# Three block loads on one ring, and TensorE's padding moved from ahead of its dummy transposes into the MLP steps

## The chip, the cores and the metric

The kernel runs on one core of a Trainium2 chip. The metric is the device time of one execution in microseconds; several executions are timed and their median is compared. The engines are named as in the profile: PE is TensorE's matmul, PEld its weight load, DVE is VectorE, ACT is ScalarE, POOL is GpSimd, and SP is SyncE, which here only issues DMAs.

## The reference

A layer normalisation feeds two branches. The first is attention with 32 heads over the last 512 rows of a key and value cache, the second a two-layer MLP with a squared ReLU, whose output goes through a SiLU and gates the first.

```
xn = layernorm(x)                                  # x: 2048 x 640
s  = softmax(q(xn) @ k.T / sqrt(128)) @ v @ wo      # 32 heads, 512 cached rows
h  = relu(xn @ w1 + b1) ** 2                        # 640 -> 1728
g  = silu(h @ w2 + b2)                              # 1728 -> 640
return x + s * g
```

## The kernel before, in words

Every product of float32 values is made of three matmuls: each operand is split into a rounded high part and the rest, and high by high, high by low and low by high are added up in PSUM. The 2048 rows are cut into four tiles of 512, and a tile into four blocks of 128 rows.

**The first tile** (`ln_first`, L226 to L334) loads its four blocks `xb` straight from `x` and normalises them before anything else can run. Block 0 is cut in two halves, one issued by SP and one by ACT. Blocks 1 to 3 go to SP, ACT and SP in turn (L242). The DMAs that an engine issues follow one another on that engine's ring. DVE takes the blocks' statistics in order (`bn`, `aggr`); the reciprocal root of blocks 0 and 1 is found together on ACT, DVE and POOL, then that of blocks 2 and 3. PE turns the blocks, 20 transposes `px` in all, so that ACT and DVE can split them into `xT`, the MLP's moving operand. Until the first of these PE has nothing to do, and runs `WARM` dummy transposes `pw` of an identity matrix.

**The MLP** runs over `steps`, one for each tile (of the first three) and each of 14 chunks of the 1728 hidden columns. `mlp_step(n)` (L471) emits first the up product of step n (`up`, or `up_half` for the one chunk of 64 columns), then the down product of step n - 1 (`down`). A full up product has 15 matmuls and so has a full down product, so that the order on PE is up 0, up 1, down 0, up 2, down 1, and so on. Within the first up product stands one more transpose, `pb`, of the biases.

**Attention** follows from about 290 us on, in 128 units of half a fetch block each, written out by a plan of due times. Its matmuls are not touched by the change.

**Slots.** PE's instructions stand in its stream in numbered slots, one each. A matmul takes two, for its weight load and for itself; a wait on a semaphore that stands on its own takes one. `pe.addr_align(BLOCK, s)` puts NOPs into the stream when the program is loaded, as many as are needed until the next instruction's slot number is s modulo `BLOCK`, 256. That is from 0 to 255 of them. There are five such places in each attention unit (`align`, L1021), and one at the very front: L249 brings the first dummy transpose to slot 88. What stands ahead of the kernel's first instruction counts too, and is not in the kernel's own text. `Ordered` (L69) keeps what is issued through `pe`, `dve`, `act`, `pool` and `sp` in program order.

Of the kernel before, what the change touches and what calls it, by code (L numbers as in the profile page):

```python
# [14 lines left out]
P = 128  # L15
NT = 512
EPS = 1e-5
WARM = 40
BLOCK = 256
FIRST_SLOT = 188  # L20
SLOTS = (0, 11, 22, 33, 42)
LEAD_SLOT = 88


@with_exitstack
def kernel(
# [20 lines left out]
    DC = D // P  # L47
# [3 lines left out]
    LN_AT = {t: (3, 7) if t == LATE else (5, 9) for t in range(1, NTILE)}  # L51
# [12 lines left out]
    chunks = [(f0, min(P, F - f0)) for f0 in range(0, F, P)]  # L64
# [4 lines left out]
    class Ordered:  # L69
# [13 lines left out]
    pe, dve, act, pool, sp = (  # L83
        Ordered(e) for e in (nc.tensor, nc.vector, nc.scalar, nc.gpsimd, nc.sync)
    )
# [8 lines left out]
    def raw(ap):  # L94
        return ap.bitcast(F32)
# [39 lines left out]
    def ln_tile(t, b):  # L135
        tag = "stage" if b < 2 else "mr"
        return xp.tile([P, D], F32, tag=tag, name=f"xb{t}_{b}")
# [3 lines left out]
    def ln_load(t):  # L141
        mv = xp.tile([P, 4, NB], F32, tag="mv", name=f"mv{t}")[:, :2, :]
        sc = xp.tile([P, 3, NB], F32, tag="sc", name=f"sc{t}")
        xn = []
        for b in range(NB):
            xb = ln_tile(t, b)
            r0 = t * NT + b * P
            nc.sync.dma_start(xb, x[r0 : r0 + P, :])
            xn.append(xb)
        LS[t] = mv, sc, xn  # L150

    def ln_block(t, b):
        mv, sc, xn = LS[t]
        st = xp.tile([P, 2, 6], F32, tag="st", name=f"st{t}_{b}", bufs=4)
        hd = D // 2
        for i in range(2):
            dve.bn_stats(st[:, i, :], xn[b][:, i * hd : (i + 1) * hd])
        dve.bn_aggr(mv[:, :, b], st)

    def ln_var(t):  # L160
        mv, sc, xn = LS[t]
        dve.tensor_scalar(sc[:, 0, :], mv[:, 1, :], EPS, None, op0=ALU.add)
        nc.scalar.activation(sc[:, 1, :], sc[:, 0, :], AF.Sqrt)

    def ln_root(t):
        mv, sc, xn = LS.pop(t)
        var, sd, y = (sc[:, i, :] for i in range(3))
        r = mv[:, 1, :]
        dve.reciprocal(y, sd)
        dve.tensor_tensor(r, y, y, op=ALU.mult)  # L170
        dve.tensor_tensor(r, r, var, op=ALU.mult)
        dve.tensor_scalar(r, r, -0.5, 1.5, op0=ALU.mult, op1=ALU.add)
        dve.tensor_tensor(r, r, y, op=ALU.mult)
        return mv
# [21 lines left out]
    def ln_chunk(t, bc, xs, c):  # L196
        xc = xp.tile([P, D], F32, tag="stage", name=f"xc{t}_{c}")[:, :NT]
        nc.sync.dma_start(xc, xT[c * P : (c + 1) * P, t * NT : (t + 1) * NT])
        dve.tensor_tensor(xc, xc, bc[0], op=ALU.subtract)
        nc.vector.tensor_tensor(xc, xc, bc[1], op=ALU.mult)  # L200
        nc.scalar.activation(xs[0][:, c, :], xc, AF.Copy)
        nc.vector.tensor_tensor(xs[1][:, c, :], xc, raw(xs[0][:, c, :]), op=ALU.subtract)
# [23 lines left out]
    def ln_first():  # L226
# [3 lines left out]
        n = NB // 2  # L230
# [7 lines left out]
        xn = [ln_tile(0, b) for b in range(NB)]  # L238
# [1 line left out]
            js = slice(i * hd, (i + 1) * hd)  # L240
            q.dma_start(xn[0][:, js], x[:P, js])
        for b in range(1, NB):  # L242
            (sp if b % 2 else act).dma_start(xn[b], x[b * P : (b + 1) * P, :])
        act.activation(warm, warm, AF.Sqrt)
        br = xp.tile([P, P], F32, tag="br", name="br", bufs=1)
        dve.memset(br, 0.0)
        BR.append(br)
        pw = psx.tile([P, NT], F32, tag="x", name="pw")
        pe.addr_align(BLOCK, LEAD_SLOT)  # L249
        for _ in range(WARM):  # L250
            pe.transpose(pw[:, :P], ident, ident)
        pts = [ps_y.tile([P, NT], F32, tag="py", name=f"px0_{c}") for c in range(DC)]
# [83 lines left out]
    def spill(t, xs, cs=slice(0, DC)):  # L336
        for i in range(2):
            pool.dma_start(xT_d[t][i][:, cs, :], raw(xs[i])[:, cs, :])

    def load_part(f, k, held=False):  # L340
        f0, n = chunks[f]
        if f % 3 and f < 9:
            if k == 0:
                BOTH[f] = keep.tile([P, 2, D], F32, tag="acc", name=f"wr{f}", bufs=2)
            w = BOTH[f][:, k, :]
        else:
            w = xp.tile([P, D], F32, tag="stw", name=f"w{k + 1}r{f}", bufs=2)
            if held:
                dve.memset(w[:, :1], 0.0)
        if k == 0:  # L350
            w = w.rearrange("p (c n) -> p c n", n=P)[:, :, :n]
            sp.dma_start(w, w1[:, f0 : f0 + n].rearrange("(c p) f -> p c f", p=P))
        else:
            for i in range(0, P, n):
                sp.dma_start(w[i : i + n, :], w2[f0 : f0 + n, :])
        PRE[f, k] = w
# [14 lines left out]
    def split_w(f, k):  # L371
        if f < FC:
            split_hi(f, PRE[f, k], k)
            split_lo(f, PRE[f, k], k, dve)
            if 9 <= f < FC - 1:
                load_part(f + 1, k)
# [37 lines left out]
    def up(t, f, xs):  # L414
        if chunks[f][1] < P:
            return up_half(t, f, xs)
        ph = ps_h.tile([P, NT], F32, tag="ph", name=f"ph{t}_{f}")
        if t == 0 and f < 2:
            order = [(c, i, j) for c in range(3) for i, j in ((0, 0), (0, 1))]
            order += [(0, 1, 0), (1, 1, 0), (3, 0, 0), (3, 0, 1), (2, 1, 0), (3, 1, 0)]  # L420
            order += [(4, 0, 0), (4, 1, 0), (4, 0, 1)]
        else:
            order = [(c, i, j) for c in range(DC) for i, j in ((0, 0), (0, 1), (1, 0))]
        for k, (c, i, j) in enumerate(order):
            nc.tensor.matmul(  # L425
                ph,
                w1s[f][i][:, c, :],
                xs[j][:, c, :],
                start=k == 0,
                stop=k == len(order) - 1,  # L430
            )
            if t == f == 0 and k == 9:
                biases()
        r = hp.tile([P, NT], F32, tag="r", name=f"r{t}_{f}")
        if t == 0 and f == rp + 1:
            split_w(f + 1, 0)
        engines(t)[1].activation(r, ph, AF.Relu, bias=b1_sb[:, f : f + 1])
        hs = [hp.tile([P, NT], F32R, tag=f"h{i}", name=f"h{t}_{f}_{i}") for i in range(2)]
        square_split(t, f, r, hs[0], hs[1])
        return hs  # L440

    def down(t, f, hs, py):
        n = chunks[f][1]
        for d in range(DC):
# [4 lines left out]
            else:  # L449
# [5 lines left out]
                )  # L455

    xs_next = ln_first()
    steps = [(t, f) for t in range(LATE) for f in range(FC)]
    XS, HS, PY, LN = {0: xs_next}, {}, {}, {}

    def gate(t, tiles):
        for d in range(DC):
# [5 lines left out]
            )  # L468
            nc.gpsimd.dma_start(g_d[t][:, d, :], sg)

    def mlp_step(n):  # L471
        if n < len(steps):
            t, f = steps[n]
            ln_stats_at, ln_chunk_at = LN_AT[t + 1]
            if t == 0 and f == 1:
                ln_load(1)
            if t == 0 and f == 6:
                LN[1] = ln_root(1)
            if t and f == ln_stats_at - 1:
                ln_load(t + 1)  # L480
            if t and f == ln_stats_at:
                for b in range(NB):
                    ln_block(t + 1, b)
                ln_var(t + 1)
                LN[t + 1] = ln_root(t + 1)
            c = f - ln_chunk_at
            if 0 <= c < DC:
                ln_chunk(t + 1, *LN[t + 1], c)
                XS[t + 1] = LN[t + 1][1]
            if t + 1 == LATE and 0 < c <= DC:  # L490
                spill(t + 1, XS[t + 1], slice(c - 1, c))
            if t == 0 and f > 0:
                split_w(f, 1)
                if f < 8:
                    for k in range(2):
                        load_part(f + 2, k)
            HS[n] = up(t, f, XS[t])
            if t == 0 and 2 <= f < 2 + NB:
                ln_block(1, f - 2)
                if f == NB + 1:  # L500
                    ln_var(1)
            if f == ln_stats_at + 2:
                LN[t + 1] = ln_rows(t + 1, LN[t + 1])
            if t > 0 and f == 1:
                spill(t - 1, XS[t - 1])
            if t == LATE - 1 and f == 3:
                spill(t, XS[t])
        if n > 0:
            t, f = steps[n - 1]
            if f == 0:  # L510
                PY[t] = [
                    ps_y.tile([P, NT], F32, tag="py", name=f"py{t}_{d}") for d in range(DC)
                ]
            down(t, f, HS.pop(n - 1), PY[t])
            if f == FC - 1 and t < LATE - 1:
                gate(
                    t,
                    lambda d: xp.tile(
                        [P, D], F32, tag=("stage", "mr")[d % 2], name=f"sg{t}_{d}"
                    )[:, :NT],  # L520
                )
# [417 lines left out]
    for n in range(steps_n):  # L939
# [24 lines left out]
    q_hi(0)  # L964
    q_lo(0)
    mlp_step(steps_n)
    gate(
        LATE - 1,
# [133 lines left out]
    for item in order:  # L1102
        kind, n = item[0], int(item[1:] or 0)
# [125 lines left out]
```

## Time and profile before

| what | value |
|---|---|
| median of 3 runs | 1960.47 us (1960.15 to 1961.4) |
| the profiled execution | 1961.36 us, of which the span from the first to the last instruction is 1959.6 us |
| PE busy | 1951.1 us, 100% of the span |
| granted TensorE clock, mean | 1.000 |
| PE's weight loads, matmuls | 8616, 8616 |
| fetches of instructions (queue q8) | 77, 1.26 MB |

The page gives, for every engine, busy time and share; the span cut in 40 slices; the chain of work that ended last; and the costliest groups. The timeline lists instructions in order of time: start, duration, engine, line, operation, and in brackets how long the engine had been idle and what ended that. Instructions of a sequencer (NOPs and waits on semaphores) show up under their source line, with the engine's name and a q: PEldq is what PE's sequencer did by itself. The view of a window gives an engine's busy time and the granted clock in it.

### The profile page before, as it was taken

The numbers are of one execution on the slowest core, as the hardware profiler recorded it, in microseconds if no ns is written. First come the engines' busy times: TensorE is split into PE (matmuls) and PEld (weight loads), VectorE is DVE, ScalarE is ACT, GpSimd is POOL, SyncE is SP. The second block draws the span as 40 slices with busy tenths as digits, with TensorE's granted clock in tenths as the row PEclk, the third lists the DMA queues.
The fourth block names the chain that finished last, engine by engine and source line by source line (L and its number), as shares of the span: only waits on it lengthen the run. The fifth ranks groups of instructions, "written<-read, shape, count | busy, mean of one in ns | idle before, by whom it ended". The sixth has DMA issues, their size and how long they took to land.

```text
span 1959.6 us, 28181 instructions
## 1 busy us (share of the span) xinstructions
PE 1951.1 (100%) x8616; PEld 1611.8 (82%) x8616; DVE 1534.8 (78%) x2638; ACT 1187.1 (61%) x2039; POOL 1375.7 (70%) x757
## 2 busy tenths in 40 slices
PE   9999999999999999999999999999999999999998
PEld 7888888888888888888888888888888888888887
DVE  5633337788888888888888878888888888888865
ACT  4432336766666666666666676666666666666643
POOL 2121226888888888888887888888888888888841
PEclk9999999999999999999999999999999999999999
DMA  5330454333333232223335433443333333333353
GB/s 182 94 119 28 183 198 128 98 93 92 92 92 92 92 92 93 92 92 93 92 92 174 145 119 108 114 114 114 113 114 114 114 114 114 98 92 92 85 189 118
DMA packets 127892, 219.13 MB, mean 112 GB/s; under 512 B 23452, under 2 KB 38086, under 8 KB 126470
## 3 DMA queue, kind: packets, MB, share of 16 engines
q1 hardware_dynamic: 124598, 202.43, 34.1%
q0 software_dynamic: 2864, 14.42, 1.8%
q8 instruction: 77, 1.26, 0.2%
q14 instruction: 65, 0.53, 0.1%
q10 hardware_dynamic: 288, 0.49, 0.1%
HBM read 193.41 MB, written 23.87 MB: 111 GB/s over the span
## 4 chain that ended last, share of the span: by engine, by line
PE 98%; DMA 1%; DVE 1%; POOL 0%; ACT 0%; issue 0%; SPq 0%; POOLq 0%; ACTq 0%
PE r L77 22%; PE pq L77 22%; PE o L77 18%; PE s L77 18%; PE ph L425 7%; PE ly L77 2%; PE py L101 2%; PE py L100 2%; PE py L102 2%; PE lu L77 2%; PE eu L77 0%; PE ph L396 0%; POOL pt L77 0%; DMA xb<-in_x_dram 0%; PE py L448 0%; PE py L447 0%
## 5 line engine op out<-in xcount | busy, mean ns | idle before, releaser
L77 POOL TENSOR_TENSOR pt<-e,pt 128x1024 fp32r<-128x1024 f32 x256 | 615.5, 2404 | 115.2 <-ACT pt L77 69.1
L77 PE MATMUL r<-ot,wo 128*128 128x512 f32 x1920 | 496.6, 389 | 0.0
L77 PE MATMUL pq<-ax,wq 128*128 128x512 f32 x1920 | 456.1, 389 | 0.0
L77 PEld LDWEIGHTS pq<-ax,wq 128*128 128x128 f32 x1920 | 360.3, 188 | 75.3 <-DVE q L77 0.4
L77 PEld LDWEIGHTS r<-ot,wo 128*128 128x128 f32 x1920 | 360.4, 188 | 74.9
L77 PE MATMUL o<-pt,wv 128*128 128x512 f32 x1536 | 369.7, 389 | 0.1
L77 PE MATMUL s<-q,wk 128*128 128x512 f32 x1536 | 369.1, 389 | 0.1
L77 DVE TRANSPOSE_TENSOR_REDUCE rdm<-s 128x16 f32<-128x512 f32 x512 | 346.5, 711 | 6.2 <-PE s L77 6.0
L77 ACT ACTIVATE e<-e 128x1024 f32<-128x1024 f32 x256 | 269.8, 1054 | 125.5 <-DVE e L77 82.0
L77 PEld LDWEIGHTS o<-pt,wv 128*128 128x128 f32 x1536 | 288.1, 188 | 60.9 <-POOL pt L77 1.2
L77 PEld LDWEIGHTS s<-q,wk 128*128 128x128 f32 x1536 | 288.1, 188 | 60.5 <-DVE e L77 0.7
L77 DVE TENSOR_TENSOR e<-s,bm 128x512 f32<-128x512 f32 x512 | 312.2, 664 | 7.6 <-DMA bm<-m_d 7.1
L77 POOL TENSOR_TENSOR su<-e,e 128x1024 f32<-128x1024 f32 x128 | 309.1, 2415 | 0.0
L77 ACT ACTIVATE pt<-e 128x1024 fp32r<-128x1024 f32 x256 | 272.0, 1063 | 6.9
L77 DVE TENSOR_TENSOR acc<-r,acc 128x512 f32<-128x512 f32 x300 | 203.4, 678 | 12.9 <-PE r L77 12.6
L77 ACT ACTIVATE rdm<-rdm 32x64 f32<-32x64 f32 x384 | 97.8, 255 | 181.5 <-DVE rdm L77 178.4
L77 DVE TRANSPOSE_TENSOR_REDUCE rds<-su 128x32 f32<-128x1024 f32 x128 | 158.3, 1237 | 0.3 <-POOL su L77 0.3
L77 DVE TENSOR_TENSOR ot<-o,ot 128x512 fp32r<-128x512 f32 x128 | 88.5, 691 | 86.1 <-ACT ot L77 86.1
L77 ACT ACTIVATE q<-pq 128x512 fp32r<-128x512 f32 x128 | 76.7, 600 | 111.5 <-PE pq L77 111.4
L425 PE MATMUL ph<-xT,w1s 128*128 128x512 f32 x585 | 139.5, 390 | 0.0
L425 PEld LDWEIGHTS ph<-xT,w1s 128*128 128x128 f32 x585 | 109.5, 188 | 23.5 <-DVE xT L77 0.9
L77 ACT ACTIVATE rds<-rds 32x32 f32<-32x32 f32 x384 | 89.7, 234 | 63.0 <-DVE rds L77 59.7
(137 smaller groups left out, 1940.9 us busy)
## 6 DMA issues: line engine op xcount, KB each, us to landing
bm<-m_d SPq DMA_DIRECT2D x128, 256.0 KB, 3.2
bs<-s_d SPq DMA_DIRECT2D x128, 256.0 KB, 4.0
qr<-in_wq_dram SPq DMA_DIRECT2D x64, 320.0 KB, 4.5
or<-in_wo_dram SPq DMA_DIRECT2D x64, 320.0 KB, 4.7
kr<-in_kT_dram SPq DMA_DIRECT2D x64, 256.0 KB, 4.3
vr<-in_v_dram SPq DMA_DIRECT2D x64, 256.0 KB, 4.4
xT_d<-xT POOLq DMA_DIRECT2D x6, 1280.0 KB, 8.0
ax<-xT_d SPq DMA_DIRECT2D x4, 1280.0 KB, 10.6
```

The costliest lines, as they stand in the source:

```text
L77: ins = method(*args, **kwargs)
L100: nc.tensor.matmul(ps, ah, bh, start=first and i == 0, stop=False)
L101: nc.tensor.matmul(ps, ah, bl, start=False, stop=False)
L102: nc.tensor.matmul(ps, al, bh, start=False, stop=last and i == n - 1)
L425: nc.tensor.matmul(ph, w1s[f][i][:, c, :], xs[j][:, c, :], start=k == 0, stop=k == len(order) - 1,)
```

## The change

Blocks 2 and 3 are now issued by SP right behind block 1, so that ACT issues only its half of block 0. The alignment ahead of the dummy transposes is gone, and `WARM` is 38 in place of 40. In steps 1 to 23 of the MLP there is a new alignment behind the step's up product and ahead of the down product. The slot that it asks for is a start, `LEAD_SLOTS`, plus two slots for each matmul that `up` and `down` and the row transposes have emitted by then, plus `LEAD_PADS` for each step.

```
-WARM = 40
+WARM = 38
-LEAD_SLOT = 88
+LEAD_SLOTS, LEAD_PADS = 171, 2
...
         for b in range(1, NB):
-            (sp if b % 2 else act).dma_start(xn[b], x[b * P : (b + 1) * P, :])
+            sp.dma_start(xn[b], x[b * P : (b + 1) * P, :])
...
-        pe.addr_align(BLOCK, LEAD_SLOT)
         for _ in range(WARM):
             pe.transpose(pw[:, :P], ident, ident)
...
+    LEAD_N = 23
+
+    def lead_slot(n):
+        ups = sum(2 * (2 if chunks[steps[k][1]][1] < P else 3) * DC for k in range(n + 1))
+        downs = sum(2 * (2 if chunks[steps[k][1]][1] < P else 3) * DC for k in range(n - 1))
+        turns = 2 * sum(1 for k in range(n + 1) if steps[k][1] == LN_AT[steps[k][0] + 1][0] + 2)
+        return (LEAD_SLOTS + ups + downs + turns + LEAD_PADS * n) % BLOCK
...
             if t > 0 and f == 1:
                 spill(t - 1, XS[t - 1])
+            if 0 < n <= LEAD_N:
+                pe.addr_align(BLOCK, lead_slot(n))
             if t == LATE - 1 and f == 3:
                 spill(t, XS[t])
```

## The prediction

> **What bounds the kernel now.** I read the page first: busy times and the chain that ended last.
>
> ```profile
> span 1959.6 us, 28181 instructions
> ...
> PE 1951.1 (100%) x8616; PEld 1611.8 (82%) x8616; DVE 1534.8 (78%) x2638; ACT 1187.1 (61%) x2039; POOL 1375.7 (70%) x757
> ...
> PE 98%; DMA 1%; DVE 1%; POOL 0%; ACT 0%; issue 0%; SPq 0%; POOLq 0%; ACTq 0%
> ```
>
> PE is the bound, almost without a gap. Whatever keeps PE waiting is added to the time as it is, and little is to be gained. The waits of PE's weight loads from 20 us to the end say how little:
>
> ```profile
> PEld o L77 <- POOL pt L77: 1.2, 3, 0.5
> PEld s L77 <- DVE e L77: 0.7, 2, 0.6
> PEld py L101 <- DVE h L77: 0.5, 1, 0.5
> PEld pq L77 <- DVE q L77: 0.4, 1, 0.4
> ```
>
> That is 2.8 us in seven waits (us in total, times, longest). The rest of what PE loses lies before its first real work, in the first 20 us. The timeline there:
>
> ```profile
> 2.55 6.51 PE L77 MATMUL pw<-ident 128*128 128x128 f32 x40 [2.55 <-issue]
> 3.54 0.89 DVE L77 BATCH_NORM_STATS2 st<-xb 128x6 f32<-128x320 f32 x2 [2.50 <-DMA xb<-in_x_dram]
> ...
> 4.62 0.06 DVE L77 MEMSET w1r<- 128x1 f32 x1
> ...
> 5.56 0.89 DVE L77 BATCH_NORM_STATS2 st<-xb 128x6 f32<-128x320 f32 x2 [0.88 <-DMA xb<-in_x_dram]
> ...
> 8.51 0.83 ACT L77 ACTIVATE xb<-xb,mv 128x640 f32<-128x640 f32 x1 [0.76 <-POOL mv L77]
> ...
> 9.39 0.53 PEld L77 LDWEIGHTS px<-ident,xb 128*128 128x128 f32 x5 [0.56 <-ACT xb L77]
> ```
>
> DVE has block 0's statistics done at 4.68, waits 0.88 us for block 1 to land, and the chain from there (statistics, root, scale) frees PE's first transposes at 9.39. The 40 dummies end at 9.06, 0.33 us ahead of that.
>
> **The loads.** What the DMAs moved in the first 14 us, in 40 slices of 0.35 us:
>
> ```profile
> GB/s 0 0 0 0 0 124 234 304 410 377 307 388 410 410 410 293 129 110 227 344 364 399 355 135 89 219 168 209 401 399 354 322 337 389 432 395 432 351 359 402
> ```
>
> The sixth to the sixteenth slice move 1283 KB (their sum, 3667 GB/s, by 0.35 us), so all four blocks of 328 KB land close together at about 5.6 us. In one ring's order block 1 is complete when 656 KB have moved. The slices reach 614 KB at 3.85 us and 750 KB at 4.2, so it lands at about 4.0 to 4.3, before DVE asks for it at 4.68. The 0.88 us go. Block 0 no longer shares with block 2 and may come up to 0.4 us sooner too. Against it: one ring might move less than two, and then nothing is gained. Bounds 0 to 1.3 us, taken 0.9, since from slice 20 on SP alone moves as much. Blocks 2 and 3 cannot come later than 5.8 us, where the four are complete, and DVE takes block 2 at 5.9 in the new order. ACT's issue of block 2 (0.4 us) goes and SP's of block 3 comes as late again; SP's next one, the first weights, waits for DVE's memset at 4.62 anyway, so nothing waits for either.
>
> **The padding in front.** What PE's sequencer did by itself, from its rows under line 77 up to 20.5 us, and then over the whole span:
>
> ```profile
> L77 PEldq NOP  x23: 13/13/13, 0.8 to 2.5; - x23
> L77 PEldq EVENT_SEMAPHORE  x5: 51/51/51, 7.0 to 14.8; - x5
> ```
> ```profile
> L77 PEldq NOP  x2528: 13/13/13, 0.8 to 1855.1; - x195
> ```
>
> 23 NOPs stand ahead of the dummies, from 0.8 to 2.5 us (the load behind them starts at 2.52): 0.074 us each. Without them the dummies start when POOL has made the identity, at about 1.35, and 38 of them end near 7.6 to 8.0. That is before the transposes, now due at 8.5, so the front padding costs nothing before, and its removal and two dummies fewer bring nothing.
>
> **Where the new alignments fall.** This decides. The 23 NOPs brought the stream to slot 88, so the kernel's first free slot was 88 - 23 = 65. Nothing in the change alters what stands ahead of it. Now count the slots to the first new alignment, step 1's, between the second up product and the first down product: 65, then 76 for 38 dummies, 40 for 20 transposes, 30 for the first up product, 2 for `pb`, 30 for the second, and 5 for the semaphore waits in the row above: 248. The slot asked for is 171 + 30 + 30 (`ups` for steps 0 and 1) + 0 + 0 + 2 = 233. The stream is 15 slots beyond it, and the next slot 233 is 241 NOPs away. Counted on in the same way, the other 22 alignments need one or two each, 41 together, and attention starts at the same slot as before, one block of 256 later.
>
> The 41 cost 41 x 0.074 = 3.0 us of PE's sequencer and I cost them at nothing: the other 2505 NOPs of the row above lie among the matmuls of attention, where all of PE's waits are the 2.3 us above. What covers them is the sequencer's lead, which these rows show at the place of the first alignment:
>
> ```profile
> L100 PEld LDWEIGHTS py<-h,w2s x5: 187/188/188, 19.8 to 22.9; 128*128 128x128 f32 x5
> L100 PEldq EVENT_SEMAPHORE  x1: 51/51/51, 16.4 to 16.4; - x1
> ```
> ```profile
> L425 PEld LDWEIGHTS ph<-xT,w1s x20: 187/188/192, 15.3 to 19.6; 128*128 128x128 f32 x20
> ```
> ```profile
> 23.77 3.56 PE L425 MATMUL ph<-xT,w1s 128*128 128x512 f32 x15
> ```
>
> The semaphore wait in front of the first down load was passed at 16.4 us, the load itself ran at 19.8. A matmul takes (3.56 - 0.39) / 14 = 0.226 us, so the sequencer was 15 matmuls, 3.4 us, ahead. If that cover were gone everywhere the 41 would cost their 3.0 us.
>
> 241 NOPs are 241 x 0.074 = 17.8 us, five times the lead. Bounds for one NOP, from the row's rounding, 0.070 and 0.078, hence 16.9 to 18.8.
>
> **The sum.** The sequencer comes to the padding at 16.4 - 0.9 = 15.5 us, leaves it at 33.3, and the first down load runs at 33.4 in place of 19.8: +13.6. PE has run dry at 18.9, and stands for 14.5 us. Behind it all of PE's work, and so everything else, is later by the same amount. DVE, ACT and POOL go on meanwhile, so the wait for `h` is over:
>
> ```profile
> 20.00 0.39 PE L100 MATMUL py<-h,w2s 128*128 128x512 f32 x1
> ...
> 20.44 0.50 PE L101 MATMUL py<-h,w2s 128*128 128x512 f32 x1
> ...
> 20.77 0.40 PE L102 MATMUL py<-h,w2s 128*128 128x512 f32 x1
> ```
>
> These three started 0.77 us apart where 0.45 would do: -0.3. Last, the clock. Rows of the dummies before and after 6.4 us, PE's last matmuls, and the end of the span:
>
> ```profile
> L77 PE MATMUL pw<-ident 128*128 128x128 f32 x18 | 4.1, 422 | 2.5 <-issue 2.5
> ```
> ```profile
> L77 PE MATMUL pw<-ident 128*128 128x128 f32 x22 | 2.6, 277 | 0.0
> ```
> ```profile
> 1947.76 6.74 PE L77 MATMUL ly<-lh,l2w 128*128 128x512 f32 x29
> ```
> ```profile
> 1956.00:1959.60 3.60, 0.00 (x0) 0.00 (x0) 0.68 (x2) 0.00 (x0) 0.00 (x0) 0.92 0.21 73
> ```
>
> The first 18 dummies follow each other at (4.1 - 0.42) / 17 = 0.216 us, the other 22 at (2.6 - 0.28) / 21 = 0.110: for about 4.0 us from its first matmul PE ran at half speed. The last matmul ends at 1954.5, and in the last 3.6 us the granted clock averages 0.92: at half speed for 0.6 us, so it fell some 4.5 us after the last work. An idle time of 14.5 us is thus long enough for it to fall, and 4.0 us at half speed cost about 4.0 x 0.49 = 1.9 us. Bounds: 0, and 3.3 for a cold time as long as all 40 dummies' 6.5.
>
> [...]
>
> 13.6 - 0.3 + 1.9 = +15.2 us. Against the profiled execution, 1961.36 (1.76 us of it outside the span), that is 1976.6; it stood 0.9 above the median of 1960.47, against which I forecast 1975.7.
>
> **The rivals.**
> The padding is short (the other side). It turns on 15 slots: had the stream at step 1 reached slot 233 or less, the alignment would take 0 to 2 NOPs or so, as the other 22 do, and what is left is the gain of 0.9: 1959.6, no change that can be told. For it: what stands ahead of the kernel was counted in a profiled execution, and the timed ones may have 15 fewer; the pads of the other steps are all small, as if the start of 171 had been taken for such a stream. Against it: nothing in the trace shows a first slot other than 65.
> The padding is passed faster than the front's NOPs were. Between the waits at 14.8 and 16.4 the sequencer passed 43 slots in 1.65 us, 0.038 each. At that pace 241 take 9.2 us, the first down load runs at 24.8, +5.0 - 0.3, and with the clock 1967.1; jumped over at once they would leave 1959.6. Against it: the front's row, three times as slow or more, for the same instruction.
> [...]
> The clock stays up: 1973.8. One ring brings nothing: 1976.6. Both lie within the likeliest case's range.
>
> **How the numbers follow.** The long padding at the front's pace has 0.83. The short padding has 0.12; padding passed faster 0.04, half of it slower and half unchanged; 0.01 is left for a gain elsewhere. 0.2% is 3.9 us, about what a measurement of this kernel can tell from no change, and a gain of 0.9 is far below that, so faster 0.01, same 0.14, slower 0.85. The low end takes 0.9 less for the NOPs, 0.4 more for the loads and no clock loss, 1972.5; the high end 1.0 more for the NOPs, 0.9 for no gain from the loads, 1.4 for the clock and a run like the slowest shown (0.9), 1979.9. The short padding is left outside, as the 2 in 10 allow.
>
> **What would show it.** Under line 77 no NOPs before the dummies, which start near 1.35 us; DVE's idle before block 1's statistics gone; transposes from about 8.5. In the MLP 282 NOPs (under line 77, the helper's), 241 of them in one run from about 15.5 to 33.3 us; PE idle from about 19 to 33.4, the granted clock at half behind that for some 4 us, and from there the same spacing as before. 2505 or 2506 NOPs in attention, 78 fetches on q8. It would be wrong if the kernel's first slot is 50 or lower, which shows as a first alignment of no more than two NOPs.

## The result and the profile after

The changed kernel takes 1976.16 us in the median of five runs (1975.17 to 1977.99), the kernel before 1960.97 in five (1960.15 to 1961.4). The ratio is 1.0078, with an interval from 1.0064 to 1.0092, or 15.2 us more. The profiled execution took 1975.39 us. From the page of the changed kernel:

```profile
span 1973.6 us, 28437 instructions
...
PE 1952.4 (99%) x8614; PEld 1614.1 (82%) x8614; DVE 1535.1 (78%) x2638; ACT 1186.9 (60%) x2039; POOL 1375.1 (70%) x757
...
q8 instruction: 78, 1.28, 0.2%
...
PE 98%; issue 1%; ACT 0%; DMA 0%; DVE 0%; POOL 0%; SPq 0%; POOLq 0%
```

The engines' work is the same, the span is 14.0 us longer, and 1% of the chain has become "issue", time in which an engine waited for nothing that the profile shows. The waits of PE's weight loads from 20 us to the end have one new row, and it is the largest by far:

```profile
PEld py L100 <- issue: 14.6, 1, 14.6
PEld pq L77 <- DVE q L77: 0.4, 1, 0.4
PEld o L77 <- POOL pt L77: 0.3, 1, 0.3
```

The timeline shows the place: the second up product ends, then nothing, then the first down product.

```profile
1.37 6.96 PE L77 MATMUL pw<-ident 128*128 128x128 f32 x38 [1.37 <-POOL mv L77]
...
4.65 0.49 DVE L77 BATCH_NORM_STATS2 st<-xb 128x6 f32<-128x320 f32 x1
...
6.10 0.49 DVE L77 BATCH_NORM_STATS2 st<-xb 128x6 f32<-128x320 f32 x1
...
8.68 0.53 PEld L77 LDWEIGHTS px<-ident,xb 128*128 128x128 f32 x5 [0.59 <-ACT xb L77]
...
14.66 4.81 PE L424 MATMUL ph<-xT,w1s 128*128 128x512 f32 x20
...
33.65 0.29 PEld L100 LDWEIGHTS py<-h,w2s 128*128 128x128 f32 x1 [14.60 <-issue]
33.68 0.77 PE L100 MATMUL py<-h,w2s 128*128 128x512 f32 x1 [14.21 <-issue]
...
38.96 3.57 PE L424 MATMUL ph<-xT,w1s 128*128 128x512 f32 x15
```

What PE's sequencer did meanwhile stands under line 77, here from 14 to 36 us:

```profile
L77 PEldq NOP  x241: 13/13/13, 15.7 to 33.5; - x121
```

It executed 241 NOPs in a row, (33.5 - 15.7) / 240 = 0.074 us each, while PE ran out of matmuls at 19.5. Over the whole span there are 2788 of them:

```profile
L77 PEldq NOP  x2788: 13/13/13, 15.7 to 1869.1; - x200
```

From 14 to 280 us, that is in the MLP, there are 282:

```profile
L77 PEldq NOP  x282: 13/13/13, 15.7 to 177.0; - x141
```

That is 241, then 41 in the other 22 alignments, and 2506 in attention. The granted clock (the column behind POOL's) in four stretches of the changed kernel:

```profile
14.60:19.40 4.80, 4.80 (x22) 3.68 (x20) 2.25 (x4) 1.78 (x3) 2.05 (x2) 1.00 0.85 285
19.40:33.60 14.20, 0.07 (x1) 0.00 (x0) 3.62 (x5) 2.68 (x5) 1.04 (x1) 0.65 0.29 93
33.60:37.20 3.60, 3.52 (x8) 2.81 (x9) 0.00 (x0) 0.00 (x0) 0.00 (x0) 0.50 0.02 5
37.60:42.00 4.40, 4.40 (x21) 3.62 (x20) 0.00 (x0) 0.00 (x0) 0.00 (x0) 1.00 0.00 0
```

It fell during the idle time (a mean of 0.65 over 14.2 us is 9.9 us at half, so from about 23.7 us on), and PE's first 3.6 us behind it ran at half.

So the loss adds up. The first down matmul starts at 33.68 in place of 20.00: +13.7. From there to the next up product are 5.28 us in place of 3.77: +1.5, which is 1.9 us of slow clock less the 0.4 that PE lost there before. That product starts 15.2 us later (38.96 against 23.77), and the medians are 15.2 apart. The two profiled executions are only 14.0 apart, because the one of before had more short waits in attention (2.3 us of its loads' against 0.7). Such waits differ from one execution to the next in the kernels below too.

### The profile page after: what moved, and what is told of

It is laid out like the page before. It is cut to its first block, busy times and chain, and to the rows that moved or that the text cites. A ratio compares the mean times of both kernels' runs of the same rounds, so it can differ in the third digit from the quotient of the medians.

```text
span 1973.6 us, 28437 instructions
## 1 busy us (share of the span) xinstructions
PE 1952.4 (99%) x8614; PEld 1614.1 (82%) x8614; DVE 1535.1 (78%) x2638; ACT 1186.9 (60%) x2039; POOL 1375.1 (70%) x757
## 4 chain that ended last, share of the span: by engine, by line
PE 98%; issue 1%; ACT 0%; DMA 0%; DVE 0%; POOL 0%; SPq 0%; POOLq 0%
PE pq L77 22%; PE r L77 22%; PE o L77 18%; PE s L77 18%; PE ph L424 6%; PE ly L77 2%; PE py L100 2%; PE py L101 2%; PE py L102 2%; PE lu L77 2%; PE eu L77 1%; PE ph L395 0%; DMA xb<-in_x_dram 0%; PE py L446 0%; PE py L447 0%
```

## The experiments

Kernels that ran together share runs of the kernel before on the same chip. Its median was 1960.8 us beside the first alignment of one NOP, the jumped padding, the padding alone and one ring alone, 1960.78 beside the runs of 41, 65 and 129 NOPs, and 1960.58 beside the last two.

**A first alignment of one NOP.** The start of the slots is raised so far that the stream's 248th slot is not beyond it.

```
-LEAD_SLOTS, LEAD_PADS = 171, 2
+LEAD_SLOTS, LEAD_PADS = 188, 1
```

> The changed kernel with a start of 188 and one slot a step in place of 171 and two, so that the first alignment takes 1 NOP and not 241; ring, dummies and all the rest as changed. The theory (the 241 NOPs are the whole loss): no idle of PE between the second up product and the first down product, and 1960.3 us, that is the kernel before less the 0.7 us by which its transposes started earlier in the changed kernel (8.68 for 9.39). The rival that the spread padding costs by itself (23 places, each with the sequencer held up): 1 to 3 us above that, 1961 to 1963. The rival that the loads on one ring or the missing front padding cost something later: PE's waits behind 20 us grow above the 2.8 us of before.

Measured: 1959.73 us (1959.29 to 1960.36, 11 runs), ratio to the kernel before 0.9994 (0.9986 to 1.0003). The timeline and the waits of PE's loads from 20 us on:

```profile
19.22 0.39 PE L100 MATMUL py<-h,w2s 128*128 128x512 f32 x1
```
```profile
PEld o L77 <- POOL pt L77: 0.9, 3, 0.4
PEld pq L77 <- DVE q L77: 0.4, 1, 0.4
```

Two numbers in the source take back the whole 16.4 us. The spread padding costs nothing that shows, and nothing later has grown. The median is 0.6 us below the expected 1960.3 and 1.1 below the kernel before, but the interval holds 1, so this can't be told from no change.

**The padding jumped over.** Slots and stream as in the changed kernel, 241 NOPs included, but beyond 8 NOPs a branch goes around them.

```
-                pe.addr_align(BLOCK, lead_slot(n))
+                pe.addr_align(BLOCK, lead_slot(n), max_nops=8)
```

> The changed kernel with a limit of 8 NOPs for each new alignment, above which the padding is jumped over by a branch: the slots stay as they are, 241 NOPs are in the stream but are not executed. The theory (PE starves because its sequencer executes 241 NOPs at 74 ns): the branch is covered by the sequencer's lead of 3.4 us, no idle there, 1960.3. The rival that it is the place in the stream that costs (the jump leaves one block of 256 for the next, whose fetch has to be waited for): a wait of PE of 1 to 4 us at that place, 1961 to 1964.

Measured: 1960.09 us (1959.59 to 1961.54, 10 runs). PE's sequencer from 14 to 24 us, and the first down matmul:

```profile
L77 PEldq COMPARE_BRANCH  x1: 303/303/303, 15.6 to 15.6; - x1
```
```profile
19.18 0.39 PE L100 MATMUL py<-h,w2s 128*128 128x512 f32 x1
```

The jump took 0.3 us and PE did not notice it. So neither the 241 slots in the stream nor the block that they fill cost anything that shows; executing the NOPs did. The other alignments' 41 NOPs were executed here too (from 14 to 280 us), at no cost that shows:

```profile
L77 PEldq NOP  x41: 13/13/13, 22.3 to 161.1; - x41
```

**Runs of 41, 65 and 129 NOPs.** On the kernel with the short first padding; what is missing to 256 is jumped over one step later, so that all later slots stay (here for 65).

```
+                extra, most = (64, 255) if n == 1 else (0, 8)
-                pe.addr_align(BLOCK, lead_slot(n))
+                pe.addr_align(BLOCK, (lead_slot(n) + extra) % BLOCK, max_nops=most)
```

> The kernel with the short first padding, with 41 NOPs in place of 1 at the first alignment; the rest of the 256 slots is jumped over at the second one, so that all later slots stay. The theory (NOPs cost what goes beyond the sequencer's lead): it comes to them at 15.6 us and leaves them 41 x 0.074 = 3.0 later, at 18.7, ahead of the first down load's 19.0; no idle of PE there, and the time of the short padding, 1959.7. The rival that each NOP is paid for: 1962.7.

> As the run of 41, with 65. The theory: 65 x 0.074 = 4.8, so the first down load is at 20.5 in place of 19.0, and the wait of 0.3 for h behind it is gone: 1.5 of idle, +1.2 on all of PE's later work, no fall of the clock: 1960.9. Each NOP paid for: 1964.5.

> As the run of 41, with 129. The theory: 9.5 us, the first down load at 25.2, idle 6.2, +6.0 on the later work without the clock: 1965.7. The clock fell 4.5 us after the last work at the end of the span before, so it should fall here too, near the end of the idle time, and cost 1.6 to 3.3 more: 1967.3 to 1969.0. [...]

Measured: 1959.95 us (1959.44 to 1960.47, 10 runs), 1961.05 (1960.62 to 1961.44, 10 runs) and 1967.88 (1967.05 to 1968.14, 6 runs), each within 0.3 of what the lead predicts or inside its range. The NOPs and the first down matmul, kernel by kernel:

```profile
L77 PEldq NOP  x41: 13/13/13, 15.6 to 18.7; - x41
```
```profile
19.22 0.39 PE L100 MATMUL py<-h,w2s 128*128 128x512 f32 x1
```
```profile
L77 PEldq NOP  x65: 13/13/13, 15.6 to 20.5; - x65
```
```profile
20.66 0.47 PE L100 MATMUL py<-h,w2s 128*128 128x512 f32 x1 [1.32 <-ACT r L77]
```
```profile
L77 PEldq NOP  x129: 13/13/13, 15.9 to 25.5; - x129
```
```profile
25.68 0.77 PE L100 MATMUL py<-h,w2s 128*128 128x512 f32 x1 [6.07 <-issue]
```

41 NOPs end before the load is due, and the matmul starts at 19.22 as with one. 65 end after it, and PE waits for the sequencer alone; the row names ACT as the releaser, but that had long been done. With 129 the idle time is 6.1 us, and the clock is in play:

```profile
19.60:25.60 6.00, 0.01 (x1) 0.00 (x0) 3.61 (x5) 2.62 (x5) 1.07 (x1) 0.80 0.46 132
25.70:30.00 4.30, 4.30 (x10) 3.42 (x11) 0.00 (x0) 0.00 (x0) 0.00 (x0) 0.50 0.34 117
30.20:34.00 3.80, 3.80 (x19) 3.12 (x18) 0.00 (x0) 0.00 (x0) 0.00 (x0) 1.00 0.02 4
```

A mean of 0.80 over 6.0 us is 2.4 us at half, so it fell 3.6 us after the last matmul. Behind the gap 4.3 us ran at half, some 2 us lost. 25.68 - 19.22 - 0.3 + 2.1 = 8.3, and the median is 8.2 above that of the short padding. All six runs lie above 1967, where 1965.7 was expected without the clock, so it fell in each. No run shows the 1.6 at the low end of the expected price; the shortest half clock behind a gap here, 3.6 us in the changed kernel, is 1.8 by the factor of 0.49. Nor does the clock always wait for the 4.5 us that the expectation takes from the end of the span before. At the end of the run of 41 the last matmul ended at 1953.07, and in the 4 us from 1953 on the clock averages 0.76. That is half speed for 1.9 us, so the clock fell 2.0 us after the last matmul:

```profile
1944.75 8.32 PE L77 MATMUL ly<-lh,l2w 128*128 128x512 f32 x36
```
```profile
1953.00:1957.00 4.00, 0.07 (x1) 0.00 (x0) 1.61 (x4) 0.84 (x2) 0.00 (x0) 0.76 0.36 131
```

**The padding alone**, on two rings:

```
-            sp.dma_start(xn[b], x[b * P : (b + 1) * P, :])
+            (sp if b % 2 else act).dma_start(xn[b], x[b * P : (b + 1) * P, :])
```

> The changed kernel with the loads on two rings again, so the padding's part alone. The theory: 241 NOPs as before, everything 0.7 us later: 1976.9. If the ring's gain is lost in the padding (the sequencer comes to it by something other than the data of the first tile), the time is that of the changed kernel, 1976.2.

Measured: 1976.73 us (1975.52 to 1979.52, 4 runs). The padding alone is the whole loss. Whether the ring's gain survives it stays open, since the four runs spread over both forecasts, 1976.9 and 1976.2. The profiled run is the slowest of the four, and shows two things that made it so: blocks 1 and 2 came late, DVE waited for them, and the transposes began at 10.21; and behind the idle time the half clock lasted 6.2 us.

```profile
7.63 0.49 DVE L77 BATCH_NORM_STATS2 st<-xb 128x6 f32<-128x320 f32 x1 [0.56 <-DMA xb<-in_x_dram]
...
10.21 0.53 PEld L77 LDWEIGHTS px<-ident,xb 128*128 128x128 f32 x5 [1.89 <-ACT xb L77]
```
```profile
35.10:41.30 6.20, 6.12 (x15) 4.79 (x15) 0.00 (x0) 0.00 (x0) 0.00 (x0) 0.50 0.01 3
```

**One ring alone**, on the kernel before:

```
-            (sp if b % 2 else act).dma_start(xn[b], x[b * P : (b + 1) * P, :])
+            sp.dma_start(xn[b], x[b * P : (b + 1) * P, :])
```

> The kernel before with blocks 1 to 3 on SP's ring and nothing else. The theory: DVE's 0.88 us of waiting for block 1 go, block 2 comes late instead (landed at 6.07 in the changed kernel), the dummies end at 9.06 where the transposes could start at 8.68, but the second block's transposes wait for ACT until 9.6 anyhow, so the first matmuls of the MLP come 0.7 us earlier: 1960.3. The rival that the dummies' end holds the transposes up for good: 0.3 to 0.4 earlier only, 1960.6. The rival that one ring gains nothing: 1961.0.

Measured: 1960.43 us (1959.5 to 1960.93, 11 runs), ratio 0.9998 (0.9989 to 1.0007). That is between the rivals, and not told from any of them by time. The trace says more:

```profile
2.53 7.23 PEld L77 LDWEIGHTS pw<-ident 128*128 128x128 f32 x40 [2.53 <-issue]
9.73 1.34 PEld L77 LDWEIGHTS px<-ident,xb 128*128 128x128 f32 x12
```

In this execution the weight loads of the 40 dummies took 7.23 us, against 6.30 in the kernel before. By the spacings of 0.216 and 0.110 us that is nine more of them at half speed, so the clock rose later, and the dummies held up transposes whose data was ready about a microsecond earlier (DVE took the reciprocal for blocks 0 and 1 at 6.42, against 6.51 in the changed kernel, whose transposes began at 8.68). The first down matmul started at 19.84, only 0.16 earlier than before and not 0.7. So with the loads on one ring the 23 NOPs ahead of the dummies are not always free.

**The padding's move without the ring, and without the long run**: the short first padding with the loads on two rings (the edit shown for the padding alone).

> The kernel with the short first padding, with the loads on two rings as before, so the padding's move without its long run and without the ring. The theory (the ring brings 0.7 and the front padding's removal the rest of what the short padding gained on the kernel before, 1.1): 1960.4, with DVE waiting 0.9 for block 1 and transposes at 9.4. If the ring is all, 1960.8; if the ring is nothing, 1959.7.

Measured: 1959.95 us (1959.4 to 1960.99, 11 runs). In its profile:

```profile
5.34 0.89 DVE L77 BATCH_NORM_STATS2 st<-xb 128x6 f32<-128x320 f32 x2 [0.66 <-DMA xb<-in_x_dram]
```
```profile
9.18 0.53 PEld L77 LDWEIGHTS px<-ident,xb 128*128 128x128 f32 x5 [0.79 <-ACT xb L77]
```

The transposes began at 9.18 and not at the expected 9.4, because block 1 landed 0.2 earlier than in the profile of the kernel before. By medians the ring brings 0.2 us (1959.73 against 1959.95; 0.4 when each is set against the kernel before that ran beside it), and the front padding's removal, with two dummies fewer, 0.6. That is the other way round than expected, though the first transposes come 0.6 earlier with the ring (8.58 with the same padding). All these differences are within the intervals. Nor does the microsecond lie at the front alone: in the profile of the short padding the transposes come 0.8 earlier than before (8.58 for 9.39), and the short waits of PE's loads in attention come to 1.3 us in place of 2.3. How it is shared stays open.

**The root ahead of block 2's statistics**, on the kernel with the short first padding:

```
-        bn(n, 0)
         dve.reciprocal(Y[0], SD[0])
+        bn(n, 0)
```

> The kernel with the short first padding, and in the first tile DVE takes the reciprocal for blocks 0 and 1 ahead of the first half of block 2's statistics. The theory (what the loads on one ring gained less than the 0.9 forecast is block 2's late landing, for which DVE waited between the root and its reciprocal): the transposes start at 8.5 or earlier in every execution, up to 0.2 before the 8.7 of the changed kernel, and the time is 1959.5, which can't be told from 1959.7. If block 2 has nothing to do with it, the transposes stay at 8.6 to 8.7 or come later, since the statistics fill a wait for ACT.

Measured: 1959.67 us (1959.27 to 1960.26, 11 runs).

```profile
6.26 0.17 DVE L77 RECIPROCAL sc<-sc 128x2 f32<-128x2 f32 x1 [0.16 <-ACT sc L77]
6.34 0.87 DVE L77 BATCH_NORM_STATS2 st<-xb 128x6 f32<-128x320 f32 x2
```
```profile
8.46 0.53 PEld L77 LDWEIGHTS px<-ident,xb 128*128 128x128 f32 x5 [0.49 <-ACT xb L77]
```

The transposes start at 8.46, the earliest of all profiles here, although block 0 came later than in the others. From DVE's instruction ahead of the root to the reciprocal it is 0.33 us (5.93 to 6.26), in place of 0.70 in the changed kernel. So block 2's place in DVE's order did hold back blocks 0 and 1. In time it can't be told from the kernel with the short padding.

## Why the prediction was right

**The slot count** (65 from the 23 NOPs, then 248 against a target of 233) carried everything, and it was exact: 241 NOPs in one run, 41 more in the MLP, 2506 in attention, 78 fetches. The 15 slots fewer on which the rival of the short padding turned were not seen in the timed runs either, since all five lie 14 us or more above the median of the kernel before, like the profiled one.

**The price of a NOP.** 0.074 us, as in the front; the rivals of faster passing are out. The jumped padding is the one of them that can be had on purpose, and it costs nothing that shows.

**The lead.** PE ran dry at 19.5 instead of the 18.9 at which its next load was due (PE was 0.7 us early and not 0.9, and the last matmul takes 0.4 us itself). The runs of 41 and 65 NOPs bracket the lead between 3.0 and 4.8 us (41 and 65 times 0.074), around the 3.4 taken.

**The sum.** +13.6 was +13.7, -0.3 for the wait for `h` was the 0.4 shown above, the clock's +1.9 was 1.9. Together 15.2, as forecast; the forecast of 1975.7 is 0.5 low because the median before rose from 1960.47 to 1960.97 with more runs. That the sum agrees to a tenth is in part luck: the half clock behind the gap lasted 3.6 us in the changed kernel's profile and 6.2 in that of the padding alone, which by the factor of 0.49 moves its term by 1.3 us.

**The loads**, the term that was off. The forecast took 0.9 us; the transposes came 0.7 earlier (8.68 for 9.39). DVE's wait for block 1 did go. What failed is that blocks 2 and 3 "cannot come later than 5.8 us". Block 2 was issued at 1.67 and landed 4.4 us later; the chain that ended last, up to the first transposes, goes through it:

```profile
1.67 4.41 DMA xb<-in_x_dram
...
6.10 0.49 DVE st L77
```

DVE reached its statistics before it had landed, and behind them stands the reciprocal for blocks 0 and 1. DVE's instruction ahead of the root and the reciprocal show the size, first in the kernel before and then in the changed one:

```profile
6.73 0.17 DVE L77 TENSOR_SCALAR sc<-mv 128x2 f32<-128x2 f32 x1
...
7.21 0.15 DVE L77 RECIPROCAL sc<-sc 128x2 f32<-128x2 f32 x1
```
```profile
5.81 0.17 DVE L77 TENSOR_SCALAR sc<-mv 128x2 f32<-128x2 f32 x1
...
6.51 0.15 DVE L77 RECIPROCAL sc<-sc 128x2 f32<-128x2 f32 x1
```

The first comes 0.92 us earlier, as forecast, the second only 0.70. The order with the root first agrees, but it takes block 2's statistics out of the way as well as the wait for them, so the 0.2 us of late landing are read from these rows alone. The possible gain of 0.4 from block 0 was nothing: DVE took it at 3.60 in place of 3.54.

**The padding in front costs nothing before**: true of the profiled execution, whose dummies ended at 9.06, and not shown for every one. With one ring the clock rose later (7.23 us of weight loads for the dummies, against 6.30), and the first transpose behind the same 40 dummies was loaded only at 9.73; in the kernel before that would be 0.3 us behind its data at 9.39, but no profile of it shows that. If so, some tenths of a microsecond are missing in a term that was put at zero. The changed kernel's 38 dummies were to end at 7.6 to 8.0 and ended at 8.33 (1.37 and 6.96 in the row above), still ahead of the transposes.

## What to carry to other kernels

An alignment has a direction: a stream that is one slot beyond its target pays almost a full block (here 15 slots beyond it cost 241 NOPs, in blocks of 256), and the place where it pays may be far from the edit that added the slot. Count slots from a known one before choosing a target, or give the alignment a limit above which it jumps; the jump took 0.3 us here, and the lead of PE's sequencer hid it. What PE's sequencer spent on NOPs cost nothing up to its lead (41 NOPs, 3.0 us, were free here) and its full price beyond (65 NOPs, 4.8 us, put the first down matmul at 20.66 in place of 19.22, so 3.4 us were covered), and behind the gap of 6.1 us that 129 NOPs left, 4.3 us at half speed cost some 2 us on top.

## What the runs showed of the hardware that was not expected

How long the half clock lasts behind a gap varies much: 3.6 us in the changed kernel, about 4.4 with 129 NOPs, 6.2 in the profiled run with the padding alone, for idle times of 14.2, 6.1 and 14.2 us. It does not grow with the idle time in these three. With what fell into the idle time the changed kernel's clock stood at half for 13.65 us, from 23.79 to 37.44:

```profile
23.70:23.79 0.09, 0.00 (x0) 0.00 (x0) 0.00 (x0) 0.00 (x0) 0.00 (x0) 1.00 0.86 341
23.79:37.44 13.65, 3.76 (x9) 3.02 (x10) 0.00 (x0) 0.00 (x0) 0.00 (x0) 0.50 0.16 51
37.45:42.00 4.55, 4.55 (x21) 3.72 (x21) 0.00 (x0) 0.00 (x0) 0.00 (x0) 1.00 0.00 0
```

Where the spread comes from, no run here set out to show.

The full clock came with transposes alone: the dummies are transposes with nothing else on PE, and in the kernel before they sped up from 0.216 to 0.110 us each after 4.0 us.

How soon the full rate came varies too. By these two spacings the 38 dummies of the short padding, 5.74 us in all, ran at half for 2.9 us, and those of the changed kernel, 6.96 us in all, for 5.3.

```profile
1.38 5.74 PE L77 MATMUL pw<-ident 128*128 128x128 f32 x38 [1.38 <-POOL mv L77]
```
